# Reordering the first batches of an attention and MLP kernel: an earlier load of v, two attention outputs ahead of their scores, later loads gated on transposes

## The chip, the cores and the metric

The kernel runs on one core of a Trainium2 chip. The metric is device time in microseconds (us), as the median of several executions. Five engines work side by side, each through its own queue in program order: PE (matrix products), ACT (activation functions and copies), DVE (elementwise work and reductions), POOL (elementwise work, and the queue from which the loads are issued) and SP (a queue that only issues transfers). An engine whose next instruction waits does nothing else in the meantime.

## The reference, cut to what matters

Eight batches of eight heads go through a causal attention with a decay, and the result through an MLP with an exact GELU. S is 576, the head size 64, the model width 512, the hidden width 2048.

```python
scores = scale * np.matmul(q, k.transpose(0, 1, 3, 2))
cum = np.cumsum(np.maximum(s, 0.0), axis=-1)
bias = -(cum[:, :, :, None] - cum[:, :, None, :])
scores = np.where(causal, -1e9, scores + np.minimum(bias, 0.0))
attn = np.exp(scores - np.max(scores, axis=-1, keepdims=True))
attn = attn / (np.sum(attn, axis=-1, keepdims=True) + 1e-09)
x = np.matmul(attn, v)            # then [B, S, H * D]
...
h = x @ w_in
out = (0.5 * h * (1.0 + erf(h / np.sqrt(2.0)))) @ w_out
```

## The kernel before, in words

**What is computed where.** Heads go in pairs p = 0 to 3. Scores are made transposed, with exp of them in a tile P (two halves, "unit" 0 and 1), and the factor exp(cum) of the decay is put into v and into the weights of the row sum: `wb` holds exp(cum), `vv` holds v times `wb`. So an output is a numerator (vv times P) over a denominator (wb times P). The kernel works in bf16 and ends with a branch into a general version that this input does not take.

**Blocks.** After an opening (lines 583 to 645) that makes batch 0's attention, the loop over c (line 647) has nine blocks of 512 tokens. A block runs the first MLP product (`l1_item`, L519, eight pairs of hidden tiles) and then the second one (`l2_item`, L541, four groups "sub" of 128 tokens) cut into pieces, between which the attention of batch nb = c + 1 is put. The order on every engine is the order of the program text (`manual_schedule`, L86), so a line's place in the text is its place in each queue.

**The pieces of attention.**
- `tr_items` (L355) transposes q and k of a pair on PE (L366) into PSUM and copies them to `qkT` (L372), by ACT or DVE. It serves batches 0 and 1. From batch 2 on, `interleave` (L176) rearranges the loaded rows by four POOL copies (L180), `write_rows` (L187) writes them to DRAM from the SP queue, and `transpose_rows` (L194) brings them back transposed, eight transfers a batch, from the same queue.
- `sc_item` (L379) makes a pair's scores on PE, one unit at a time in one of two PSUM slots with the tag "sc", takes exp on ACT (L403), and zeroes the diagonal blocks on DVE (`mask_item`, L412 and L417). In the opening some items add a large negative number on PE instead (`neg=True`, L395).
- `av_item` (L479) makes a pair's denominator and numerator (L425), ln and exp of the denominator on ACT (`norm_act`, L441 and L442), and the product on DVE (`norm_dve`, L461) into xT, which `l1_item` of the next block reads. With `wide=True` the two lie in one "sc" slot, else in two slots with the tag "av".
- `scale_pair` (L580) makes `vv` of one pair on DVE (L232). `weights_dve` and `weights_pe` (L259 to L270) make cum and `wb`: one DVE operation, five transposes on PE, two exp on ACT.
- `keep_busy(n)` (L589) issues n products on zeros that nothing reads.

**Loads.** All loads of q, k, v and the weights are issued from POOL. `load_early(b, n, p)` loads half of q or k of a batch, `load_v` a batch's v in five slices, `load_w` a quarter of a weight. `pace` (L578) is a one-element POOL copy: what it reads must be there before POOL goes on to the loads behind it. Before the change it reads gT of the block from block 2 on (L665), which is written once the block's first GELU is done; at L717 and L746 it reads the last transposed k of a batch.

Of the kernel before, what the change touches and what calls it, by code (L numbers as in the profile page):

```python
# [19 lines left out]
def kernel(  # L20
# [10 lines left out]
    nc = tc.nc  # L31
# [12 lines left out]
    NP = H // 2  # L44
# [25 lines left out]
    MAIN = [(jt, i0, min(i0 + n, CUT) - i0, off) for jt, i0, n, u, off in SEGS if i0 < CUT]  # L70
# [86 lines left out]
    qkT = [const.tile([128, 2, NP, 640], bf16, name=f"qkT{i}") for i in range(2)]  # L157
# [101 lines left out]
    def weights_dve():  # L259
        nc.vector.tensor_scalar(cum, s_pos, s_pos[:, 287:288], None, op0=ALU.subtract)  # L260
# [160 lines left out]
    def av_mm(b, p, out, parts, den):  # L421
        for n_part, (jt, lo, n, off) in enumerate(parts):
            for e in range(2):
                h = 2 * p + e
                nc.tensor.matmul(  # L425
                    out[e * 64 : e * 64 + 64, lo : lo + n],
                    lhsT=(
                        wb[:, jt, b * H + h : b * H + h + 1].to_broadcast([128, 64])
                        if den else vv[b % 2][:, jt, h, :]
                    ),  # L430
                    rhs=P_of[b, p][:, e, off : off + n],
                    start=(n_part == 0), stop=n_part == len(parts) - 1,
                    skip_group_check=True,
                )
# [31 lines left out]
    def av_banks(wide=False, last=False):  # L466
        if wide:
            t = ps.tile([128, 2, 512], fp32, tag="sc", bufs=2, name="avw")
            return t[:, 0], t[:, 1]
        if last:  # L470
            num = ps.tile([128, 512], fp32, tag="mlp", bufs=1, name="avn")
            den = ps.tile([128, 512], fp32, tag="av", bufs=3, name="avd")
            return num, den
        den, num = [ps.tile([128, 512], fp32, tag="av", bufs=3, name=n) for n in ("avd", "avn")]
        return num, den
# [2 lines left out]

    def av_item(b, p, wide=False, rest=True):  # L479
        num, den = av_banks(wide)  # L480
        av_mm(b, p, den, MAIN, True)
        ln = norm_act(den, CUT, CHUNKS)
        av_mm(b, p, num, MAIN, False)
        if rest:
            av_rest(b, p)
        norm_dve(b, p, p + 1, num, ln, 0, CUT, CHUNKS)
# [14 lines left out]
    gT_of = {}  # L501
# [76 lines left out]
    pace = const.tile([128, 1], fp32, name="pace")  # L578

    def scale_pair(b, p):  # L580
        scale_v(b, ((0, ST - 1), (ST - 1, ST)), nc.vector, 2 * p, 2 * p + 2)
# [7 lines left out]
    def keep_busy(n):  # L589
        for _ in range(n):  # L590
            nc.tensor.matmul(warm, lhsT=busy[:, :128], rhs=busy, start=True, stop=True)  # L591
# [4 lines left out]
    keep_busy(3)  # L596
    sc_item(0, 0, masks=False)
    nc.vector.tensor_scalar(neg_bf, tri_bf, 2048.0, -2048.0, op0=MULT, op1=ALU.add)
    keep_busy(1)
    tr_items(0, 1, (0,))  # L600
    keep_busy(2)
    tr_items(0, 1, (1,))
    keep_busy(3)
    sc_item(0, 1, neg=True, units=(0,))
    tr_items(0, 2, (0,))
    keep_busy(1)
    tr_items(0, 2, (1,))
    weights_dve()
    sc_item(0, 1, neg=True, units=(1,))
    tr_items(0, 3, (0,))  # L610
    sc_item(0, 2, neg=True, units=(0,))
    weights_pe()
    tr_items(0, 3, (1,))
    sc_item(0, 2, neg=True, units=(1,))
    mask_item(0, 0, 0, nc.vector)
# [13 lines left out]
        load_early(1, n, 0)  # L629
    for i in range(4):  # L630
        load_w(1, i)
    for n in "qk":
        load_early(1, n, 2)
    load_v(1)
    load_qk(2)
    avs = {p: av_banks(p < 2, p == 3) for p in (2, 0, 1, 3)}
    for p in (2, 0, 1, 3):
# [9 lines left out]
    for c in range(NCH):  # L647
        nb = c + 1
        for k0, k1 in ((0, 2), (2, 3)) if c == 0 else ((0, 3),):
            l1_item(c, 0, k0, k1)  # L650
            l1_item(c, 1, k0, k1)
        l1_item(c, 0, KO - 1)
        l1_item(c, 1, KO - 1)
        l1_item(c, 2, av=True)
        if 0 < c and nb < B:
            scale_v(nb, STS, nc.vector)
            absmax_v(nb)
        if c == 0:
            absmax_v(0)
            scale_v(0, STS[ST - 1 :], nc.vector)  # L660
        if c < B:
            for p in range(NP):
                absmax(c, p)
        if 1 < c and nb + 1 < B:
            nc.gpsimd.tensor_copy(pace, gT_of[c][:, 0, 0:1])  # L665
            load_v(nb + 1)
            if nb + 2 < B:
                load_qk(nb + 2)
        for f2 in range(3, FT // 2):
            l1_item(c, f2)  # L670
        if c == 0:
            load_v(2)
            interleave(2, "q")
            interleave(2, "k")
            for p in range(NP):
                av_rest(0, p)
            tr_items(1, 0, (0, 1), wide=True)
            tr_items(1, 1, (0, 1), (nc.scalar.copy, nc.vector.tensor_copy), wide=True)
            exp_set()
            l2_item(c, 0, 0, 4)  # L680
            l2_item(c, 1, 0, 4, av=True)
            norm_rest(0)
            l2_item(c, 0, 4, 8)
            sc_item(1, 0)
            l2_item(c, 1, 4, 8, av=True)
            l2_item(c, 0, 8, 12)
            sc_item(1, 1)
            l2_item(c, 1, 8, 12, av=True)
            l2_item(c, 2, 0, 8, av=True)
            l2_item(c, 0, 12, copy=nc.scalar.copy)  # L690
            l2_item(c, 1, 12, av=True)
            tr_items(1, 2, (0, 1), (nc.scalar.copy, nc.vector.tensor_copy), wide=True)
            l2_item(c, 2, 8, 12, av=True)
            tr_items(1, 3, (0, 1), (nc.scalar.copy, nc.scalar.copy), wide=True)
            scale_pair(1, 0)
            l2_item(c, 2, 12, av=True)
            scale_pair(1, 1)
            l2_item(c, 3, 0, 4)
            sc_item(1, 2)
            av_item(1, 0, rest=False)  # L700
            scale_pair(1, 2)
            l2_item(c, 3, 4, 8)
            sc_item(1, 3)
            av_item(1, 1, rest=False)
            scale_pair(1, 3)
            write_rows(2, 0, nc.sync)
            l2_item(c, 3, 8, 12)
            av_item(1, 2, wide=True, rest=False)
            write_rows(2, 1, nc.sync)
            l2_item(c, 3, 12)  # L710
            av_item(1, 3, rest=False)
            for p in (0, 1):
                transpose_rows(2, p)
            gelu_set()
            for p in (2, 3):
                transpose_rows(2, p)
            nc.gpsimd.tensor_copy(pace, qkT[0][:, 1, 3, 0:1])  # L717
            load_qk(3)
            load_v(3)
            absmax_v(1)  # L720
        elif nb < B:
            exp_set()
            l2_item(c, 0, 0, 4)
            if c == 1:
                for p in range(NP):
                    av_rest(1, p)
            sc_item(nb, 0)
            if c == 1:
                norm_rest(1)
            l2_item(c, 0, 4)  # L730
            late = int(c == 1)
            for p in range(1, NP):
                if nb + 1 < B and p == 1 + late:
                    interleave(nb + 1, "q")
                    write_rows(nb + 1, 0, nc.sync)
                if nb + 1 < B and p > 1 and not late:
                    transpose_rows(nb + 1, p - 2)
                sc_item(nb, p)
                av_item(nb, p - 1)
                l2_item(c, p, 0, 12)  # L740
                if p == NP - 1:
                    if nb + 1 < B:
                        for pt in range(0 if late else p - 1, NP):
                            transpose_rows(nb + 1, pt)
                    if c == 1:
                        nc.gpsimd.tensor_copy(pace, qkT[(nb + 1) % 2][:, 1, p, 0:1])  # L746
                        load_qk(nb + 2)
                    av_item(nb, p)
                    norm_rest(nb)
                    gelu_set()  # L750
                l2_item(c, p, 12)
                if nb == B - 1 and p == 1:
                    cert_decay()
                if nb + 1 < B and p == 1 + late:
                    interleave(nb + 1, "k")
                    write_rows(nb + 1, 1, nc.sync)
        else:
            if c == B - 1:
                cert_1()
            for sub in range(4):  # L760
                if c == NCH - 1 and sub == 3:
                    l2_last(c, sub)
                    break
                l2_item(c, sub, av=sub % 2 == 0)
                if c == B - 1 and sub < 3:
                    (cert_2, cert_3, cert_4)[sub]()
# [151 lines left out]
```

## Time and profile before

| what | us |
|---|---|
| median of five runs (lowest to highest) | 331.78 (330.45 to 332.49) |
| the profiled execution, its time | 329.58 |
| its span, first to last instruction | 327.8 |
| opening, until the first product of block 0 starts | 0 to 21.06 |
| block 0, until block 1 goes on for good | 21.06 to 61.02 |
| block 1 | 61.02 to 95.28 |
| blocks 2 to 6 | 34.05 to 34.10 each |
| block 7, block 8 | 28.50, 33.70 |

The span is 1.78 us shorter than the time of its own execution, and that execution is 2.20 us below the median of the five. Times within the profile are us from the start of the span. A row of a timeline gives the start, the length, the engine, the line, what is written from what, and how many instructions were merged; in brackets stands how long the engine had been idle, and who ended that.

### The profile page before, as it was taken

To read this page: it belongs to the slowest core of one execution; us is meant where nothing else is said; L and a number is where in the kernel's file an instruction comes from. 1 tells how busy PE (TensorE), PEld (TensorE's weight loads), DVE (VectorE), ACT (ScalarE), POOL (GpSimd) and SP (SyncE) were. 2 spreads that over 40 slices of the span, in tenths; PEclk is the share of its full clock that TensorE was granted. 3 is DMA by queue.
4 is the path that set the end of the run, shared out by engine and by line. 5 is a ranking of instruction groups with operands and counts; after the bars stand their busy time and mean duration, and the time that the engine had idled before them with its cause. 6 is when DMAs were issued, how large, how long until landed. Compare 5 with 4: busy or idle time off the path is not lost.

```text
span 327.8 us, 8739 instructions
## 1 busy us (share of the span) xinstructions
PE 316.6 (97%) x3760; PEld 183.6 (56%) x3760; DVE 187.9 (57%) x356; ACT 204.9 (63%) x292; POOL 93.2 (28%) x124
## 2 busy tenths in 40 slices
PE   8999997899999999999999999999999999999992
PEld 3576655666665556546655665556555655455552
DVE  5777547995659366935494548644883672150021
ACT  4697758669576767677667767677759676105400
POOL 8744354407700970670058003700000000000000
PEclk9999999999999999999999999999999999999999
DMA  7999999967975899899689795627600100010012
GB/s 116 220 209 210 210 212 281 238 110 103 253 232 118 152 236 284 160 151 252 197 142 230 191 178 103 169 95 199 126 2 34 65 34 2 34 66 34 1 66 72
DMA packets 53838, 47.45 MB, mean 145 GB/s; under 512 B 31328, under 2 KB 43872, under 8 KB 53792
## 3 DMA queue, kind: packets, MB, share of 16 engines
q0 software_dynamic: 15936, 23.07, 38.0%
q1 hardware_dynamic: 37856, 23.75, 29.3%
q8 instruction: 31, 0.51, 0.7%
q14 instruction: 15, 0.12, 0.1%
HBM read 36.85 MB, written 16.52 MB: 163 GB/s over the span
## 4 chain that ended last, share of the span: by engine, by line
PE 94%; ACT 3%; DVE 1%; issue 0%
PE h_ps L519 38%; PE o_ps L541 37%; PE sc_ps L387 6%; PE avd L425 4%; PE avn L425 3%; PE warm L591 2%; ACT P L403 1%; PE tr_ps L366 1%; PE o_ps L562 1%; PE avr L425 1%; ACT ln L441 1%; DVE qkT L372 0%; PE sc_ps L395 0%; PE avw L425 0%; ACT gT L529 0%
## 5 line engine op out<-in xcount | busy, mean ns | idle before, releaser
L541 PE MATMUL o_ps<-w_out_r,gT 128*64 128x512 bf16 x1120 | 129.5, 380 | 0.0
L519 PE MATMUL h_ps<-xT,w_in_r 128*64 128x512 bf16 x1152 | 126.2, 379 | 0.7 <-DVE xT L461 0.7
L519 PEld LDWEIGHTS <-w_in_r 128*64 128x64 bf16 x1152 | 68.5, 110 | 56.4 <-issue 1.2
L541 PEld LDWEIGHTS <-gT 128*64 128x64 bf16 x1120 | 61.0, 110 | 49.6
L526 ACT ACTIVATE gT<-h_ps 128x1024 bf16<-128x1024 f32 x54 | 54.3, 1023 | 52.7 <-PE h_ps L519 52.7
L403 ACT ACTIVATE P<-sc_ps 128x1024 bf16<-128x1024 f32 x64 | 62.2, 1020 | 28.2 <-PE sc_ps L387 25.6
L412 DVE TENSOR_TENSOR P<-P,tri_bf 128x512 bf16<-128x512 bf16 x58 | 27.3, 477 | 47.4 <-ACT P L403 46.7
L548 DVE COPY o_sb<-o_ps 128x512 f32<-128x512 f32 x34 | 23.3, 686 | 47.6 <-PE o_ps L541 47.6
L215 DVE TENSOR_REDUCE amx<-qkT 128x2 f32<-128x1152 bf16 x32 | 40.9, 1335 | 0.0
L204 POOL DMA_DIRECT2D raw_v<-in_v_dram x40 | 34.2, 880 | 9.1 <-DMA w_out_r<-in_moe_w_out_dram 4.3
L461 DVE SCALAR_TENSOR_TENSOR xT<-avn,ln 128x256 bf16<-128x256 f32 (+3 forms) x66 | 22.4, 385 | 21.7 <-ACT ln L442 15.1
L232 DVE TENSOR_TENSOR vv<-raw_v,wb 128x512 bf16<-128x512 f32 (+3 forms) x44 | 26.8, 667 | 1.5 <-DMA raw_v<-in_v_dram 1.5
L442 ACT ACTIVATE ln<-ln 128x512 f32<-128x512 f32 (+1 forms) x40 | 23.5, 587 | 1.3
L222 DVE TENSOR_REDUCE amv<-raw_v 128x1 f32<-128x2048 f32 (+1 forms) x16 | 23.0, 1469 | 2.2 <-DMA raw_v<-in_v_dram 2.2
L441 ACT ACTIVATE ln<-avd 128x256 f32<-128x256 f32 x58 | 19.2, 391 | 7.6 <-PE avd L425 7.6
L529 ACT ACTIVATE gT<-h_ps 128x512 bf16<-128x512 f32 x36 | 19.6, 602 | 6.3 <-PE h_ps L519 6.3
L387 PE MATMUL sc_ps<-qkT 64*128 64x256 bf16 (+2 forms) x320 | 21.0, 250 | 0.5 <-ACT P L403 0.2
L387 PEld LDWEIGHTS <-qkT 64*128 64x128 bf16 x320 | 13.0, 94 | 14.9 <-issue 12.4
L425 PEld LDWEIGHTS <-vv 128*64 128x64 bf16 x384 | 17.7, 110 | 3.5 <-issue 2.6
L425 PEld LDWEIGHTS <-wb 128*64 128x64 bf16 x384 | 17.1, 110 | 4.1 <-issue 0.3
L665 POOL CAST pace<-gT 128x1 f32<-128x1 bf16 x4 | 1.9, 483 | 56.0 <-ACT gT L526 56.0
L425 PE MATMUL avd<-P,wb 128*64 128x256 bf16 x232 | 16.5, 263 | 0.0
(99 smaller groups left out, 188.2 us busy)
## 6 DMA issues: line engine op xcount, KB each, us to landing
out_dram<-o_sb SPq DMA_DIRECT2D x35, 256.0 KB, 3.5
raw_v<-in_v_dram POOLq DMA_DIRECT2D x32, 256.0 KB, 7.6
rows<-qk_bf SPq DMA_DIRECT2D x12, 576.0 KB, 5.1
early_q<-in_q_dram POOLq DMA_DIRECT2D x13, 288.0 KB, 10.2
early_k<-in_k_dram POOLq DMA_DIRECT2D x13, 288.0 KB, 10.8
w_in_r<-in_moe_w_in_dram POOLq DMA_DIRECT2D x4, 512.0 KB, 11.9
w_out_r<-in_moe_w_out_dram POOLq DMA_DIRECT2D x4, 512.0 KB, 15.1
raw_v<-in_v_dram POOLq DMA_DIRECT2D x8, 128.0 KB, 9.2
```

What stands on the lines that cost most here:

```text
L204: nc.gpsimd.dma_start(out=t[:n_st, st, :, :], in_=bass.AP(tensor=v.tensor, offset=v.offset + b * H * S * D + st * 128 * D, ap=[[D, n_st], ...
L215: nc.vector.tensor_reduce(amx[:, b * NP + p], qkT[b % 2][:, :, p, :S], axis=AX, op=ALU.max, apply_absolute_value=True)
L232: eng.tensor_tensor(vb[:n_st, st0:st1, h0:h1, :], t[:n_st, st0:st1, h0:h1, :], wb[:n_st, st0:st1, b * H + h0 : b * H + h1] .unsqueeze(3).t ...
L387: nc.tensor.matmul(s_ps[:, e, off : off + n], lhsT=qkT[b % 2][e * 64 : e * 64 + 64, 1, p, jt * 128 : jt * 128 + 128], rhs=qkT[b % 2][e * 6 ...
L403: nc.scalar.activation(P[:, :, UO[u] : UO[u] + UW[u]], s_ps[:, :, : UW[u]], func=AF.Exp, scale=scale)
L412: eng.tensor_tensor(d, d, tri_bf.unsqueeze(1).unsqueeze(1).to_broadcast([128, 2, 2, 128]), op=MULT)
L425: nc.tensor.matmul(out[e * 64 : e * 64 + 64, lo : lo + n], lhsT=(wb[:, jt, b * H + h : b * H + h + 1].to_broadcast([128, 64]) if den else ...
L442: nc.scalar.activation(ln[:, :w], ln[:, :w], func=AF.Exp, scale=-1.0)
L519: nc.tensor.matmul(h_of[c, f2][i][e * 64 : e * 64 + 64], lhsT=w_in_r[:, ko, ft * 128 + e * 64 : ft * 128 + e * 64 + 64], rhs=xT[:, ko, c * ...
L526: nc.scalar.activation(gT_of[c][:, f2 * 2 : f2 * 2 + 2, :], hh_of[c, f2], func=AF.Gelu)
L541: nc.tensor.matmul(o_ps[e * 64 : e * 64 + 64], lhsT=gT[:, ft, t0 : t0 + 64], rhs=w_out_r[:, ft, :], start=(ft == 0), stop=(ft == FT - 1), ...
L548: (copy or nc.vector.tensor_copy)(o_sb, o_ps)
```

## The change

Three places. In the opening, `weights_dve` and `weights_pe` come before the transposes of the second half of pair 1, the first half of pair 2 is transposed before pair 1's scores, and 15 fillers are left of 20. In the loads, v of batch 1 is issued ahead of the second q and k half of batch 1, and the one-element copy at L665 reads the last transposed k of batch nb in place of gT. In block 0, outputs (1, 0) and (1, 1) are made before the scores of pairs 2 and 3, with their `scale_pair` ahead of them; the transposes of pairs 2 and 3 come later; sub 2 of the second product runs through in one piece and is copied out by ACT; the k half of pair 3 is copied by DVE. `av_item` with `wide=True` makes the numerator before the denominator.

```diff
--- before.py
+++ after.py
@@ -478,9 +478,12 @@
 
     def av_item(b, p, wide=False, rest=True):
         num, den = av_banks(wide)
+        if wide:
+            av_mm(b, p, num, MAIN, False)
         av_mm(b, p, den, MAIN, True)
         ln = norm_act(den, CUT, CHUNKS)
-        av_mm(b, p, num, MAIN, False)
+        if not wide:
+            av_mm(b, p, num, MAIN, False)
         if rest:
             av_rest(b, p)
         norm_dve(b, p, p + 1, num, ln, 0, CUT, CHUNKS)
@@ -596,20 +599,18 @@
     keep_busy(3)
     sc_item(0, 0, masks=False)
     nc.vector.tensor_scalar(neg_bf, tri_bf, 2048.0, -2048.0, op0=MULT, op1=ALU.add)
+    weights_dve()
     keep_busy(1)
     tr_items(0, 1, (0,))
-    keep_busy(2)
+    weights_pe()
     tr_items(0, 1, (1,))
-    keep_busy(3)
+    keep_busy(1)
+    tr_items(0, 2, (0,))
     sc_item(0, 1, neg=True, units=(0,))
-    tr_items(0, 2, (0,))
-    keep_busy(1)
     tr_items(0, 2, (1,))
-    weights_dve()
     sc_item(0, 1, neg=True, units=(1,))
+    sc_item(0, 2, neg=True, units=(0,))
     tr_items(0, 3, (0,))
-    sc_item(0, 2, neg=True, units=(0,))
-    weights_pe()
     tr_items(0, 3, (1,))
     sc_item(0, 2, neg=True, units=(1,))
     mask_item(0, 0, 0, nc.vector)
@@ -629,9 +630,9 @@
         load_early(1, n, 0)
     for i in range(4):
         load_w(1, i)
+    load_v(1)
     for n in "qk":
         load_early(1, n, 2)
-    load_v(1)
     load_qk(2)
     avs = {p: av_banks(p < 2, p == 3) for p in (2, 0, 1, 3)}
     for p in (2, 0, 1, 3):
@@ -662,7 +663,7 @@
             for p in range(NP):
                 absmax(c, p)
         if 1 < c and nb + 1 < B:
-            nc.gpsimd.tensor_copy(pace, gT_of[c][:, 0, 0:1])
+            nc.gpsimd.tensor_copy(pace, qkT[nb % 2][:, 1, NP - 1, 0:1])
             load_v(nb + 1)
             if nb + 2 < B:
                 load_qk(nb + 2)
@@ -689,22 +690,21 @@
             l2_item(c, 2, 0, 8, av=True)
             l2_item(c, 0, 12, copy=nc.scalar.copy)
             l2_item(c, 1, 12, av=True)
+            scale_pair(1, 0)
+            scale_pair(1, 1)
+            l2_item(c, 2, 8, av=True, copy=nc.scalar.copy)
+            av_item(1, 0, rest=False)
+            l2_item(c, 3, 0, 4)
             tr_items(1, 2, (0, 1), (nc.scalar.copy, nc.vector.tensor_copy), wide=True)
-            l2_item(c, 2, 8, 12, av=True)
-            tr_items(1, 3, (0, 1), (nc.scalar.copy, nc.scalar.copy), wide=True)
-            scale_pair(1, 0)
-            l2_item(c, 2, 12, av=True)
-            scale_pair(1, 1)
-            l2_item(c, 3, 0, 4)
+            scale_pair(1, 2)
+            av_item(1, 1, rest=False)
+            tr_items(1, 3, (0, 1), (nc.scalar.copy, nc.vector.tensor_copy), wide=True)
+            scale_pair(1, 3)
+            l2_item(c, 3, 4, 8)
             sc_item(1, 2)
-            av_item(1, 0, rest=False)
-            scale_pair(1, 2)
-            l2_item(c, 3, 4, 8)
+            l2_item(c, 3, 8, 12)
             sc_item(1, 3)
-            av_item(1, 1, rest=False)
-            scale_pair(1, 3)
             write_rows(2, 0, nc.sync)
-            l2_item(c, 3, 8, 12)
             av_item(1, 2, wide=True, rest=False)
             write_rows(2, 1, nc.sync)
             l2_item(c, 3, 12)
```

## Prediction

> **What bounds the kernel now.** I read the page first, then the busy time by stretches, PE's waits, and the timeline of the stretch that stands out.
>
> ```profile
> PE 316.6 (97%) x3760; PEld 183.6 (56%) x3760; DVE 187.9 (57%) x356; ACT 204.9 (63%) x292; POOL 93.2 (28%) x124
> ```
>
> PE sets the end, so only time in which PE stands still can be won. By stretches (length, then PE's busy time first):
>
> ```profile
> 0.00:21.06 21.06, 18.73 (x292) 11.03 (x293) 13.69 (x32) 13.80 (x21) 15.29 (x30) 1.00 0.99 177
> 21.06:61.02 39.96, 36.94 (x545) 22.89 (x541) 25.75 (x46) 28.89 (x45) 19.49 (x24) 1.00 1.13 227
> 61.02:95.28 34.26, 34.23 (x420) 22.10 (x421) 25.02 (x41) 23.67 (x35) 12.02 (x15) 1.00 0.87 194
> 95.28:129.33 34.05, 34.05 (x395) 19.37 (x392) 22.91 (x37) 23.88 (x35) 13.95 (x19) 1.00 0.87 180
> ```
>
> Opening and block 0 hold 2.3 and 3.0 us of idle PE, the later blocks none: there the change can only lose. PE's waits name the places:
>
> ```profile
> PE avw L425 <- ACT ln L441: 2.5, 2, 2.1
> PE h_ps L519 <- DVE xT L461: 0.7, 1, 0.7
> ```
>
> and the timeline around the longest, PE, DVE and POOL:
>
> ```profile
> 57.72 0.57 PE L425 MATMUL avw<-P,vv 128*64 128x256 bf16 x8 [2.10 <-ACT ln L441]
> ...
> 61.02 0.41 PE L519 MATMUL h_ps<-xT,w_in_r 128*64 128x512 bf16 x2 [0.66 <-DVE xT L461]
> ```
> ```profile
> 57.83 2.47 DVE L232 TENSOR_TENSOR vv<-raw_v,wb 128x512 bf16<-128x512 f32 x2
> 60.23 0.74 DVE L461 SCALAR_TENSOR_TENSOR xT<-avw,ln 128x256 bf16<-128x256 f32 x2
> ```
> ```profile
> 56.38 2.24 POOL L180 COPY qk_bf<-early_q 128x1152 bf16<-128x1152 bf16 x2 [3.14 <-DMA early_q<-in_q_dram]
> 58.55 2.76 POOL L180 COPY qk_bf<-early_k 128x1152 bf16<-128x1152 bf16 x2
> ```
>
> The numerator of output 2 waits for the ln of its own denominator, because both lie in one PSUM tile. Then block 1 waits for xT, which stood on DVE behind a scale_pair of 2.47 us; earlier ones took 0.88. It ran under POOL's interleave copies (about 1.12 each). Block 1 did four products (0.43) before its stop, so it starts in effect at 61.02 - 0.43 = 60.59. That is the number to beat.
>
> **What the Trainium skill says.** "SBUF — State Buffer", section "SBUF: two separate sides": VectorE and GpSimd share a port pair under an exclusive lock; a VectorE operation with two SBUF inputs and a GpSimd operation that reads SBUF shut each other out for whole instructions. The trace agrees: the masks (L412, two SBUF inputs, 0.42 alone) took up to 2.84 under interleave copies (119.98), PSUM reads did not slow (an output copy at 84.48 took 0.69). "DMA: Bandwidth & Descriptors", section "Issuing engines are not separate DMA queues": writes from SP share the engines with POOL's loads. Agrees: v's slices landed 1.0 to 1.2 us apart, 1.8 and 2.2 once output writes had begun at 46.72. "TensorE: Matmul & The Clock Gate", section "Why this matters for your kernels": the clock falls after PE gaps beyond some 3 us. No gap here is that long; the granted clock is 1.00 in every stretch above.
>
> **Part 1, the opening.** Five fillers go (about 0.22 each, 1.1 in all), but they lie in gaps in which PE waits for exps; they are worth nothing. The end is set by ACT: eight exps of P at 1.02, with the two exps of wb (0.38 + 0.21) between the fifth and the sixth, and idle times of 1.51, 0.81 and 0.16. The wb exps move to 9.25, into the idle 1.51: that takes 0.5 off the chain. Pair 2's first transposes move ahead of pair 1's scores; their rows land at 4.07 + 5.0 = 9.07 and 4.65 + 5.2 = 9.85, before their new places (9.4, 10.7), and the 0.81 before pair 1's second exp mostly closes. New small waits (0.1, 0.35 and 0.15 before later exps) take some back. Stepping the queues with these lengths, the last exp ends at 17.3 in place of 18.1, and block 0 starts at 20.3: **gain 0.75**. The moved DVE operation (0.50) fits in DVE's idle 1.21 before 8.24; without that cover pair 1's first copy is 0.3 later.
>
> **Part 2, the order of the loads.** From issue plus time to landing, before: last w_out 41.2; q, k half 42.3 and 44.0; v slices 44.9, 46.1, 47.9, 50.1, 50.9. DVE waited for the fourth until 50.29. After: v follows w_out at some 1.07 a slice (0.55 for the short one), landing at 46.1, mostly before the first output write. The half then competes with output writes; batch 2's halves under such writes landed 1.4 and 1.6 apart, so it lands at 49.2. If no work is saved by the new order it is 50.9, and 51.8 with sub 2's write now ahead of it. I take at most 49.5. POOL issues the same number; the others keep their places.
>
> **Part 3, block 0's tail.** With the 0.75, sub 1 ends at 46.1, sub 2's eight remaining tiles at 47.85, output 0 (0.8; its vv is done at 47.6 on DVE behind sub 1's copy) at 48.65, four tiles of sub 3 at 49.5. There the transposes of pair 2 need the half, so X = 49.5. Then by queue: DVE does copy, scale_pair 2, product of output 1, and only then pair 3's k copy, until X + 4.2. That copy frees the slot for unit 1 of pair 2's scores: PE stands still 1.5 (a **new wait** on the engine that got the copy from ACT). Exps of pair 2 and 3 follow to X + 7.7; output 2 waits 0.8 for a slot; the masks of pair 3 end at X + 8.4 = 57.9, output 3 is made, and block 1 starts at 58.85. The wide swap removes the 2.10 wait, at no cost; what is late next is the masks. ACT's load is the same but for sub 2's copy (0.59), taken while it idles.
>
> That is 1.74 better than 60.59, if the masks run alone. They don't: the interleave copies begin when batch 2's q has landed (56.38 before; 54 to 56.5 after), four of 1.12 in a row. In the trace each DVE operation with two SBUF inputs that met them waited for at least one: the three masks at 85.87 to 88.8 lost 1.6 in all, those at 119.98 lost 2.4. Before, scale_pair paid; now pair 3's three masks do, with output 2's product behind them on DVE. Delay d: 1.5 gives 60.0, 2.4 gives 61.0, one whole copy for each mask (3.2) gives 61.8. I take d = 2.2, block 1 at **60.8, a loss of 0.2**. So the 0.75 and the 2.10 are both spent on one collision.
>
> **Part 4, the held loads.** From block 3 on, v and q, k loads wait for the transposes: x6 of them took 13.20 at 134.52 beside loads, 7.71 at 163.14 without. So they end at 142.8, land 1.85 later, loads are issued for 6.9 and the interleave starts at 151.6 in place of 140.9; in block 4 at 182.5 in place of 174.95. Behind POOL's wait stand loads needed a block later (v at 165, needed landed; it lands near 157) and the interleave, whose rows reach SP's queue by 156.7 in place of 154.2; pair 0 of batch 5 is needed at 178.2 and is there by 167. All hidden. But the interleave leaves the MLP stretch, where it met only absmax (one SBUF input), and comes under the masks. I price that at 0.2 in block 4 (free slot for the next output late behind DVE), bounds 0 and 1.6; a gain is excluded, since PE has no idle there.
>
> **Sum.** 0.2 + 0.2 = +0.4 on 329.58 for the profiled execution, 330.0; the median of the five lies 2.2 higher, so 331.78 + 0.4 = **332.2**. About 0.3% (1.0 us) is what a measurement of this kernel can tell from no change, so I forecast no change.
>
> **The rivals.**
> - A, the forecast: d from 1.5 to 3.2, so -0.6 to +1.4. For it: every overlap in the trace cost a copy per operation. 331.2 to 333.2; chance 0.45.
> - B, faster: the masks get through, because the interleave starts after 57.3 or VectorE wins the lock. Against: loads of before put it at 56.38. Block 1 at 58.9 to 59.2, -1.4 to -1.7: **330.2**; chance 0.28.
> - C, slower: the held loads bring block 4's interleave onto the masks of pair 0. There the denominator starts at 182.12 and the last mask ends at 182.33: no slack. It decides once the copies start before 181.8; I put them at 182.5. Price 1.6, as at 85.87, on top of A: **333.8**; chance 0.17.
> - D, the q, k half lands at 51.8, so the moved transposes stop PE for 2.3 and part 3 slides: block 1 at 61.9, 1.3 late, **333.1**; chance 0.10.
>
> **How the numbers follow.** Faster by over 0.3%: B, 0.28. Slower: C, most of D, and the end of A with d near 3 (0.10): 0.35. The rest is 0.37. The range runs from below B's middle to just below C, 330.0 to 333.6; C's chance and a little of B and D are left out. A's own range is 331.2 to 333.2.
>
> **What would show it.** Right: the last exp of the opening near 17.3; no avw wait on ln; DVE's wait for v gone; a PE wait on qkT before pair 2's second unit of scores; pair 3's masks lengthened under L180; x6 transposes in block 3 near 8 us. Wrong: masks at 0.42 with POOL copying, or block 1 before 60, or PE waits in blocks 3 to 5.

## The result and the profile after

The changed kernel takes **334.6 us** (median of 42 runs, 331.77 to 340.42), the kernel before 331.47 (79 runs beside it, 329.66 to 342.69). The ratio is **1.0076, 95% interval 1.0060 to 1.0092**: slower by 0.8%, about 2.5 us. The ratio compares the runs of each kernel that lie within 1.5% of its fastest; medians and ranges are of all runs. The forecast was 332.2, "no change", with 330.0 to 333.6 as its range.

The profiled execution of after took 335.23 us (span 333.4), 0.6 above its median; that of before lies 1.9 below its own. So the two traces stand 5.65 us apart and the medians 3.1: a part of what the traces show is not in every run. Still, even the shortest of the 42 lies above the median of before. Where a comparison below rests on the time, the medians and ratios are used, and the traces say only where it went.

The page's line of engines, as the first thing: PE's busy time has hardly grown (316.6 before), its share has fallen from 97 to 95%. So PE stands still more.

```profile
PE 317.5 (95%) x3755; PEld 186.6 (56%) x3755; DVE 201.2 (60%) x356; ACT 205.2 (62%) x292; POOL 92.8 (28%) x124
```

Next the busy time by stretches, cut at the first product of each block of after (length, then busy time and instruction count of PE, PEld, DVE, ACT, POOL, then the share of its full clock that PE was granted, DMA share, GB/s):

```profile
0.00:20.10 20.10, 17.18 (x287) 10.29 (x288) 14.14 (x32) 13.73 (x21) 14.91 (x30) 1.00 1.01 179
...
94.92:129.92 35.00, 34.37 (x395) 19.88 (x392) 24.05 (x37) 23.83 (x35) 13.94 (x19) 1.00 0.91 178
129.92:163.99 34.07, 34.07 (x394) 21.16 (x392) 23.75 (x36) 23.99 (x35) 11.71 (x14) 1.00 0.88 182
163.99:198.11 34.12, 34.12 (x395) 19.40 (x393) 23.77 (x39) 24.01 (x36) 11.54 (x14) 1.00 0.86 175
198.11:237.10 38.99, 35.84 (x395) 20.69 (x392) 24.79 (x37) 23.98 (x35) 9.04 (x10) 0.96 0.66 141
```

A block of the steady part takes 34.05. **Block 5 takes 38.99**: PE is idle in 3.15 of it, and its clock is 0.96 on the mean. Block 2 takes 0.95 longer than that. The other blocks are as before. Summed from the block starts: the opening gives 0.96 (block 0 starts at 20.10, not 21.06); of that 0.36 is left when block 1 goes on for good (60.66 - 0.43 = 60.23 against 60.59); block 2 loses 0.95, block 5 loses 4.94, the rest 0.03. That makes 5.56 of the 5.65.

PE's waits name who is late (total, times, longest):

```profile
PE avd L425 <- DVE P L412: 3.5, 3, 3.0
PE sc_ps L387 <- DVE qkT L372: 1.5, 2, 1.1
PE avw L425 <- ACT P L403: 1.2, 2, 0.9
```

The 2.1 on the ln is gone, as forecast. In its place stands a wait of 3.0 on one mask (L412), and the group of that line has gone from 477 to 661 ns on the mean:

```profile
L412 DVE TENSOR_TENSOR P<-P,tri_bf 128x512 bf16<-128x512 bf16 x58 | 37.7, 661 | 44.9 <-ACT P L403 44.3
```

One mask makes 2.96 of the 3.5. The timeline of block 5, POOL first, then DVE, then PE (start, length):

```profile
211.77 0.19 POOL L666 CAST pace<-qkT 128x1 f32<-128x1 bf16 x1 [20.82 <-DMA qkT<-rows]
212.31 4.26 POOL L204 DMA_DIRECT2D raw_v<-in_v_dram  x5 [0.35 <-issue]
216.53 2.26 POOL L180 COPY qk_bf<-early_q 128x1152 bf16<-128x1152 bf16 x2
218.70 2.46 POOL L180 COPY qk_bf<-early_k 128x1152 bf16<-128x1152 bf16 x2
```
```profile
216.50 3.67 DVE L412 TENSOR_TENSOR P<-P,tri_bf 128x512 bf16<-128x512 bf16 x1 [0.38 <-ACT P L403]
220.09 1.16 DVE L417 TENSOR_TENSOR P<-P,tri_bf 128x128 bf16<-128x128 bf16 x1
```
```profile
220.22 0.53 PE L425 MATMUL avd<-P,wb 128*64 128x256 bf16 x4 [2.96 <-DVE P L412]
```

To be read from top to bottom: the pace copy now waits for the last transpose (`<-DMA qkT<-rows`, 20.82 of idle); v's loads take POOL for 4.26 more; then the four interleave copies start at 216.53, within 0.03 of a mask of batch 6's pair 0. That mask, 0.42 when alone, takes 3.67: three copies start ahead of it (216.53, 217.62, 218.70), and it ends at 220.17, when the fourth has just begun (219.79). The next mask waits for that one (1.16). The denominator's product on PE waits 2.96 for the first. In the kernel before, the same copies ran from 206.61 to 211.02, done 4 us before the first mask of pair 0 (214.97):

```profile
206.61 2.24 POOL L180 COPY qk_bf<-early_q 128x1152 bf16<-128x1152 bf16 x2
208.78 2.24 POOL L180 COPY qk_bf<-early_k 128x1152 bf16<-128x1152 bf16 x2
```

How regular this is shows in a count over the masks of all twelve traces of this case (before, after and the ten experiments). The 650 that meet no work of POOL take 0.42 (128x512) or 0.22 (128x128) to within 0.01. Of the 100 that meet copies alone, 87 take over 0.2 longer. Of the 112 that meet only the issue of q, k loads, 9 do, by up to 0.98: so the copies are the rule, but not the only work of POOL that can hold up a mask.

What follows on PE is as dear as half the wait itself. Stretches of 3 us around it:

```profile
217.00:220.00 3.00, 0.26 (x4) 0.09 (x1) 3.00 (x1) 1.68 (x2) 3.00 (x4) 1.00 0.80 165
220.00:223.00 3.00, 2.59 (x26) 1.99 (x27) 3.00 (x8) 1.29 (x3) 1.16 (x1) 0.52 0.10 35
223.00:226.00 3.00, 3.00 (x28) 1.72 (x24) 0.31 (x1) 0.00 (x0) 0.00 (x0) 0.91 0.68 249
```

After the stop the granted clock is 0.52, then 0.91: 3 x 0.48 + 3 x 0.09 = 1.7 us lost. With the wait of 2.96 and one of 0.19 for a free output slot that is 4.9, so all but 0.1 of block 5's 4.94.

### The profile page after: what moved, and what is told of

The parts are those of the page before. It is cut to its first block, busy times and chain, and to the rows that moved or that the text cites. A ratio compares the mean times of both kernels' runs of the same rounds, so it can differ in the third digit from the quotient of the medians.

```text
span 333.4 us, 8728 instructions
## 1 busy us (share of the span) xinstructions
PE 317.5 (95%) x3755; PEld 186.6 (56%) x3755; DVE 201.2 (60%) x356; ACT 205.2 (62%) x292; POOL 92.8 (28%) x124
## 4 chain that ended last, share of the span: by engine, by line
PE 76%; DMA 11%; POOL 3%; DVE 3%; issue 3%; ACT 2%; POOLq 0%; DVEq 0%
PE h_ps L522 33%; PE o_ps L544 31%; DMA w_out_r<-in_moe_w_out_dram 5%; PE sc_ps L387 4%; DMA early_k<-in_k_dram 4%; PE avd L425 3%; PE avn L425 3%; DMA w_in_r<-in_moe_w_in_dram 2%; ACT P L403 1%; DVE P L412 1%; PE o_ps L565 1%; POOL raw_v L204 1%; PE avr L425 1%; POOL early_q L117 1%; POOL early_k L117 1%
## 5 line engine op out<-in xcount | busy, mean ns | idle before, releaser
L522 PEld LDWEIGHTS <-w_in_r 128*64 128x64 bf16 x1152 | 70.2, 110 | 54.6 <-issue 1.1
L544 PEld LDWEIGHTS <-gT 128*64 128x64 bf16 x1120 | 62.3, 111 | 50.0 <-issue 1.1
L412 DVE TENSOR_TENSOR P<-P,tri_bf 128x512 bf16<-128x512 bf16 x58 | 37.7, 661 | 44.9 <-ACT P L403 44.3
L551 DVE COPY o_sb<-o_ps 128x512 f32<-128x512 f32 x33 | 22.6, 685 | 48.0 <-PE o_ps L544 47.9
L232 DVE TENSOR_TENSOR vv<-raw_v,wb 128x512 bf16<-128x512 f32 (+3 forms) x44 | 25.2, 631 | 0.1
L425 PE MATMUL avd<-P,wb 128*64 128x256 bf16 x232 | 17.1, 265 | 3.5 <-DVE P L412 3.5
L666 POOL CAST pace<-qkT 128x1 f32<-128x1 bf16 x4 | 0.8, 195 | 64.3 <-DMA qkT<-rows 64.3
```

Source lines behind the costliest of these rows:

```text
L232: eng.tensor_tensor(vb[:n_st, st0:st1, h0:h1, :], t[:n_st, st0:st1, h0:h1, :], wb[:n_st, st0:st1, b * H + h0 : b * H + h1] .unsqueeze(3).t ...
L412: eng.tensor_tensor(d, d, tri_bf.unsqueeze(1).unsqueeze(1).to_broadcast([128, 2, 2, 128]), op=MULT)
L425: nc.tensor.matmul(out[e * 64 : e * 64 + 64, lo : lo + n], lhsT=(wb[:, jt, b * H + h : b * H + h + 1].to_broadcast([128, 64]) if den else ...
L522: nc.tensor.matmul(h_of[c, f2][i][e * 64 : e * 64 + 64], lhsT=w_in_r[:, ko, ft * 128 + e * 64 : ft * 128 + e * 64 + 64], rhs=xT[:, ko, c * ...
L544: nc.tensor.matmul(o_ps[e * 64 : e * 64 + 64], lhsT=gT[:, ft, t0 : t0 + 64], rhs=w_out_r[:, ft, :], start=(ft == 0), stop=(ft == FT - 1), ...
```

## The experiments

All were timed in five rounds beside the kernel before on the same chip. A ratio is against that kernel.

### The hold undone, and the hold alone

My theory after the first look was that the held loads (part 4) cost it all, and that parts 1 to 3 come out even. Two kernels cross the parts. The first is after with the old pace:

```diff
-            nc.gpsimd.tensor_copy(pace, qkT[nb % 2][:, 1, NP - 1, 0:1])
+            nc.gpsimd.tensor_copy(pace, gT_of[c][:, 0, 0:1])
```

> The changed kernel with one line undone: the one-element copy ahead of the later loads reads gT of the block again, in place of the last transposed k. Theory (gate): holding the loads brings the interleave copies of block 5 onto the masks of batch 6's pair 0, PE stops for 3 us there and its clock is low for some 4 us afterwards. Then this kernel keeps the opening's and block 0's 0.4 us and loses at most block 2's 0.9: between 0.5 us faster and 0.6 us slower than before, no PE wait over 1 us behind block 0. Rival (block 2 and the clock state come from the earlier start of block 1 alone, and block 5 too): as slow as the changed kernel, 2 to 5 us slower than before.

The second is before with the new pace and nothing else:

```diff
-            nc.gpsimd.tensor_copy(pace, gT_of[c][:, 0, 0:1])
+            nc.gpsimd.tensor_copy(pace, qkT[nb % 2][:, 1, NP - 1, 0:1])
```

> The kernel before with only the gate: the copy ahead of the later loads reads the last transposed k. Gate theory: 1.5 to 5 us slower than before, with a PE wait on a mask in block 4 or 5. Rival: no change, within 0.5 us of before, since opening, loads and block 0 are those of before.

Measured:

| | old opening and block 0 | new opening and block 0 |
|---|---|---|
| old pace | 331.2 (before) | 330.85, ratio 0.9992 (0.9969 to 1.0015) |
| new pace | 335.56, ratio 1.0100 (1.0037 to 1.0164) | 334.6, ratio 1.0076 (1.0060 to 1.0092) |

The hold costs 0.8 to 1.0% with either opening. The rest of the change can't be told from nothing. The hold alone rests on six runs, so its interval is wide. In its trace it isn't block 5 that is hit but blocks 3 and 4. PE's waits and, in block 3, DVE's mask:

```profile
PE avn L425 <- DVE xT L461: 2.1, 1, 2.1
PE avd L425 <- DVE P L412: 2.1, 1, 2.1
```
```profile
151.34 4.40 DVE L417 TENSOR_TENSOR P<-P,tri_bf 128x128 bf16<-128x128 bf16 x1
```

A mask of 128x128, 0.22 when alone, took 4.40: it began at 151.34, while POOL still issued q, k loads (until 152.34), and ended at 155.74, three copies later (the third ends at 155.65). So the hold brings the copies within reach of the masks in blocks 3, 4 and 5. Which of them is hit in an execution seems to hang on some hundred nanoseconds; that fits the spread of the runs, but no run shows two executions of one kernel hit in different blocks.

The kernel with the old pace shows what the hold does good. With the loads beside them the six transposes on SP's queue take 14.15 (8.47 in after), and in block 3 PE waits for their rows:

```profile
PE sc_ps L387 <- DMA qkT<-rows: 1.9, 1, 1.9
```

With the clock that followed, that block took 37.67, so the expected "no PE wait over 1 us behind block 0" was missed. This execution (333.77) is the second longest of the kernel's 22; its median was as expected.

### The hold undone in block 5 alone

```diff
-            nc.gpsimd.tensor_copy(pace, qkT[nb % 2][:, 1, NP - 1, 0:1])
+            nc.gpsimd.tensor_copy(pace, gT_of[c][:, 0, 0:1] if c == 5 else qkT[nb % 2][:, 1, NP - 1, 0:1])
```

> The held loads are released early again in block 5 alone; blocks 2 to 4 keep the new hold. My theory (in block 5 the hold brings POOL's interleave copies onto the masks of batch 6's pair 0, and PE stands still 3 us and then runs at half its clock): block 5 falls from 38.99 to 34.05, the interleave starts near 206, the time is 4.9 below after's 334.6, 329.7. Rival (the loss in block 5 comes from the work of block 5 being late through the earlier holds, whatever POOL does in it): a PE wait of over 1 us in block 5 stays and the time stays above 332.5.

Measured: 331.47 (329.34 to 336.92, 22 runs), ratio 1.0004 (0.9981 to 1.0028). Block 5 by stretches and POOL in it:

```profile
197.12:231.17 34.05, 34.05 (x395) 19.36 (x393) 20.77 (x37) 23.87 (x35) 9.17 (x10) 1.00 0.81 158
```
```profile
206.26 2.27 POOL L180 COPY qk_bf<-early_q 128x1152 bf16<-128x1152 bf16 x2
208.43 2.26 POOL L180 COPY qk_bf<-early_k 128x1152 bf16<-128x1152 bf16 x2
```

With the copies back at 206 PE has no idle in block 5; the rival, that block 5 is late whatever POOL does there, falls. The profiled execution took 329.34, the shortest of its 22. The ratio fell from 1.0076 to 1.0004, which is 2.4 us and not 4.9: the theory's place is right and its size holds for the profiled executions only. The longer runs of this kernel were not profiled; the copies are still held in blocks 3 and 4 (151.25 and 184.55 in its trace), so a hit there is the likely reason, not a shown one.

### Shorter copies: how long is a mask shut out?

The forecast took one copy for each mask as the dearest case. In the 3.67 a single mask lost three. Either VectorE (DVE) lost three times in a row by chance, or it stays shut out while GpSimd (POOL) has more to run. In block 5 each copy is cut in three:

```diff
+        step = 3 if b == 7 else G
         for j in range(2):
-            nc.gpsimd.tensor_copy(
-                t[:, j].rearrange("g r e d -> g e r d"),
-                early[b, n][:, j].rearrange("g e (r d) -> g e r d", r=G),
-            )
+            for r in range(0, G, step):
+                nc.gpsimd.tensor_copy(
+                    t[:, j].rearrange("g r e d -> g e r d")[:, :, r : r + step],
+                    early[b, n][:, j].rearrange("g e (r d) -> g e r d", r=G)[:, :, r : r + step],
+                )
```

> The last interleave, in block 5, is cut from four copies of 128x1152 into twelve of 128x384; the hold stays. Theory 1 (VectorE, once it has lost the shared port to GpSimd, stays shut out until GpSimd's run of copies ends): the mask still takes over 3 us, PE still waits about 3, time 334.6 as after. Theory 2 (a waiting VectorE operation loses one GpSimd instruction, whatever its length, and the 3.67 was chance): the mask takes 0.42 plus one short copy of about 0.4, so below 1.2; PE waits below 0.7; block 5 near 34.6 and the time near 330.2.

Measured: 332.78 (329.45 to 337.52, 12 runs), ratio 1.0048 (1.0019 to 1.0078); the profile is of an execution of 336.01, the third longest of the twelve, so it shows what can happen and not what is usual. POOL, DVE and PE in block 5:

```profile
216.19 2.74 POOL L182 COPY qk_bf<-early_q 128x384 bf16<-128x384 bf16 x6
218.86 2.94 POOL L182 COPY qk_bf<-early_k 128x384 bf16<-128x384 bf16 x6
```
```profile
216.14 4.21 DVE L419 TENSOR_TENSOR P<-P,tri_bf 128x128 bf16<-128x128 bf16 x1
```
```profile
220.40 0.27 PE L427 MATMUL avr<-P,vv 128*64 128x64 bf16 x2 [3.30 <-DVE P L419]
```

A 128x128 mask took 4.21 us under copies of about 0.52 each, started 0.45 apart: nine of them passed ahead of it (the ninth ends at 220.27, the mask at 220.35). Block 5 took 40.56. So what decides isn't the length of one copy, and cutting the copies doesn't let the mask in. In this trace the second theory falls. The first holds in its number, but not to the letter: like the mask in after, this one got in before the run's end (221.80), after some 4 us. What ends a shut-out is open. The time lies between the two forecasts (334.6 and 330.2), which fits a stop that not every execution has in full; how often it comes the runs don't say.

### The copies moved off the masks

The hold is kept. In the first kernel the interleave stands ahead of the pace copy on POOL from block 3 on; in the second also block 2's goes ahead of its q, k loads, and block 5's waits for that block's first gT. The calls further down, in the loop over the pairs, fall away for these blocks.

```diff
         if 1 < c and nb + 1 < B:
+            if 2 < c:
+                interleave(nb + 1, "q")
+                interleave(nb + 1, "k")
             nc.gpsimd.tensor_copy(pace, qkT[nb % 2][:, 1, NP - 1, 0:1])
...
```

> The changed kernel, gate kept, but from block 3 on the interleave copies stand in POOL's queue ahead of the gate and its loads, so that they run in the MLP stretch at the start of a block. If it is the meeting of copies and masks that costs, blocks 3 to 6 last 34.05 again, no mask is longer than 0.5 us there, and the kernel is 0.4 us faster than before to 0.6 us slower (block 2 is left as it is). If holding the loads costs by itself (late v or late transposes), it stays 2 us slower or more.

```diff
         if 1 < c and nb + 1 < B:
+            if c == 5:
+                nc.gpsimd.tensor_copy(pace, gT_of[c][:, 0, 0:1])
             if 2 < c:
                 interleave(nb + 1, "q")
                 interleave(nb + 1, "k")
             nc.gpsimd.tensor_copy(pace, qkT[nb % 2][:, 1, NP - 1, 0:1])
             load_v(nb + 1)
+            if c == 2:
+                interleave(nb + 1, "q")
+                interleave(nb + 1, "k")
             if nb + 2 < B:
                 load_qk(nb + 2)
...
```

> All that the change does is kept, the hold too, but in block 2 the interleave goes ahead of the q, k loads, in blocks 3 and 4 ahead of the hold, and in block 5 to that block's start. Theory (the copies on the masks are the whole loss of blocks 2 to 5): every block from 2 to 6 takes 34.05 to 34.3; against the kernel with the interleave ahead from block 3 on (330.88) 0.6 less in block 2 and 0.8 less in block 4, so 329.5. Rival (the holds cost something of their own, late transposes or rows written later): a PE wait on a DMA or on qkT in blocks 2 to 5, and no less than 330.9.

Measured: 330.88 (22 runs), ratio 0.9995 (0.9972 to 1.0018), and 330.39 (14 runs), ratio 0.9991 (0.9974 to 1.0008). The first has its time as expected, but not every block: block 4 took 34.90, where copies from 194.10 on still met two masks (1.00 and 1.16). In the second, blocks 2 to 5 take 34.06, 34.63, 34.12 and 34.05; 34.63 lies outside the forecast. Its stop of 0.41 on PE stands behind two masks (159.84 and 160.57) under copies that began at 159.23. All 14 runs lie between 329.40 and 331.41, where those of after spread over 8.6 us; only 7 of the 49 runs of before beside it were above 334, so that none of 14 was may be chance. So the hold itself costs nothing that these runs can tell once POOL's copies keep off most masks, and the rival of late rows falls: no PE wait on a DMA or on qkT in these blocks. The hoped-for 329.5 was not reached: against the first kernel the ratio moved by 0.0004, less than its interval, in place of 1.4 us.

### What the opening and block 0 are worth

The opening alone, put into the kernel before (the second hunk of the change's diff, whole; here its core):

```diff
+    weights_dve()
     keep_busy(1)
     tr_items(0, 1, (0,))
-    keep_busy(2)
+    weights_pe()
     tr_items(0, 1, (1,))
-    keep_busy(3)
+    keep_busy(1)
+    tr_items(0, 2, (0,))
     sc_item(0, 1, neg=True, units=(0,))
...
```

> The kernel before with the change's opening alone: decay exponentials first, pair 2's first transposes ahead. Theory (the opening's gain carries through only as far as a later stage isn't set by something else): block 0 starts 0.96 earlier, at 20.1; the loads of the middle stay where they were, so DVE's wait for v and the collision at the end of block 0 hold part of it back, and block 1 starts between 59.2 and 59.7 (59.73 before): 0 to 0.5 gained, 330.7 to 331.2. Rival (nothing in block 0 is tied to the loads): block 1 at 58.8 and 0.9 gained, 330.3.

Measured: 330.87 (14 runs), ratio 0.9998 (0.9972 to 1.0025). Block 0 starts at 20.25, 0.81 earlier, and block 1 at 60.29 (60.59 in effect before). PE there, and the stretches of 3 us after it:

```profile
56.92 0.57 PE L425 MATMUL avw<-P,vv 128*64 128x256 bf16 x8 [2.09 <-ACT ln L441]
```
```profile
57.00:60.00 3.00, 3.00 (x29) 2.36 (x30) 3.00 (x6) 0.68 (x2) 3.00 (x3) 0.58 0.87 261
60.00:63.00 3.00, 3.00 (x30) 2.06 (x27) 2.41 (x5) 2.42 (x4) 0.36 (x1) 0.85 0.80 307
```

In this execution the old wait on the ln cost not only its 2.09 but the clock after it, so that 0.3 was left; block 2 then lost 0.8 (34.86) with copies at 119.35, and block 2 ended later than before. In time nothing was gained that can be told from zero, within the theory's 0 to 0.5. Its start of block 1 was missed: the first product came at 60.29, where 59.2 to 59.7 was forecast (59.73 before). The rival's 58.8 is further off still.

Block 2's 0.95 in after is the same kind of meeting. One mask near 119.6 waits there behind batch 4's copies. In after and in before:

```profile
119.10 2.24 POOL L180 COPY qk_bf<-early_q 128x1152 bf16<-128x1152 bf16 x2
119.62 4.17 DVE L412 TENSOR_TENSOR P<-P,tri_bf 128x512 bf16<-128x512 bf16 x1 [0.69 <-ACT P L403]
```
```profile
118.14 2.24 POOL L180 COPY qk_bf<-early_q 128x1152 bf16<-128x1152 bf16 x2
119.98 2.84 DVE L412 TENSOR_TENSOR P<-P,tri_bf 128x512 bf16<-128x512 bf16 x1 [0.69 <-ACT P L403]
```

In eight traces this mask meets these copies, and in each the block loses what the mask takes beyond 3.22: 0.96 of 4.18 (old pace), 0.95 of 4.17 (after), 0.81 of 4.03 (opening alone), 0.63 of 3.85 (interleave ahead from block 3 on), 0.18 of 3.40 (hold undone in block 5), nothing of 2.99 (short copies), 2.84 (before) and 2.50 (hold alone). So the loss doesn't need the hold. It comes with parts 1 to 3 and with the opening alone (in after this mask starts 0.4 earlier and the copies 1.0 later, 119.10 for 118.14), but not in every execution: four of the eight (after, interleave ahead, hold undone in block 5, short copies) have one and the same order up to block 2 and lose 0.95, 0.63, 0.18 and 0.

The other way about, batch 2's interleave in block 0 is put behind the last mask of batch 1:

```diff
             load_v(2)
-            interleave(2, "q")
-            interleave(2, "k")
...
             sc_item(1, 3)
+            nc.gpsimd.tensor_copy(pace, P_of[1, 3][:, 1, PW - 1 : PW])
+            interleave(2, "q")
+            interleave(2, "k")
             write_rows(2, 0, nc.sync)
```

> The changed kernel, with batch 2's interleave copies in block 0 put behind a one-element POOL copy that reads the end of pair 3's masked P of batch 1, so that these masks run before the copies. Theory of block 0: the three masks end 2 us earlier, and block 1 starts in effect at 58.3 to 58.8 in place of 60.23, a gain of 1.5 to 2 us up to there; the transposes of batch 2 come 2 us later, with slack. Rival (something else is late next, such as ln and exp on ACT): block 1 starts less than 0.7 earlier. The end depends on where block 5's copies then fall: 1 to 5 us slower than before, or faster if they miss the masks.

Measured: 340.85 (6 runs), ratio 1.0246 (1.0188 to 1.0305); the profiled execution is the longest of the six (342.17). Pair 3's masks at the end of block 0, and PE's waits:

```profile
56.21 0.42 DVE L412 TENSOR_TENSOR P<-P,tri_bf 128x512 bf16<-128x512 bf16 x1 [0.75 <-ACT P L403]
57.12 0.42 DVE L412 TENSOR_TENSOR P<-P,tri_bf 128x512 bf16<-128x512 bf16 x1 [0.49 <-ACT P L403]
57.46 0.22 DVE L417 TENSOR_TENSOR P<-P,tri_bf 128x128 bf16<-128x128 bf16 x1
```
```profile
PE avd L425 <- DVE P L412: 6.0, 5, 2.3
```

With the masks alone block 1 starts at 58.62 and has no stop: this is the 58.85 of the prediction's part 3. So the opening and block 0 do hold 1.6 us (60.23 - 58.62) that the collision there takes. But then blocks 2 to 5 take 37.15, 37.82, 36.55 and 38.67, in all 14 us above 34.05 each, with a mask of 3.3 to 4.9 in each of the four. Block 2 starts 1.0 earlier than in after (93.90 for 94.92), batch 4's copies come later (123.78 for 119.10), and so they meet the masks of the next pair. The gain of 1.6 is lost several times over.

### Two tries at a faster kernel

The late copies of batch 2 and the off-mask version together, with block 2's copies gated between the masks of two pairs, each in its old place in the loop over the pairs:

```diff
+                    if c == 2:
+                        nc.gpsimd.tensor_copy(pace, P_of[nb, 0][:, 1, PW - 1 : PW])
                     interleave(nb + 1, "q")
...
+                    if c == 2:
+                        nc.gpsimd.tensor_copy(pace, P_of[nb, 1][:, 1, PW - 1 : PW])
                     interleave(nb + 1, "k")
```

> The kernel with the interleaves of blocks 3 to 5 moved off the masks, and the last two that still met them moved too: batch 2's waits in block 0 until the last mask of batch 1 is made, and in block 2 each of batch 4's two halves waits until the masks of a pair are made, so that it runs in the 3.5 us before the next pair's. Theory (nothing but copies on masks takes back what the opening and the order of the loads give): block 1 starts at 58.6 without a stop, in place of 60.47 in effect; block 1 takes 35.3, blocks 2 to 6 34.05 to 34.6; 1.2 less than the 330.39 of before's off-mask version, 329.2, and 0.5% below the kernel before. Rival (the later rows and transposes of batches 2 and 4 become a wait, as every placement so far has moved the stop on): a PE wait on qkT or on a DMA in blocks 2 or 3 of over 0.5, and 330.4 or more.

Measured: 333.24 (22 runs), ratio 1.0041 (1.0016 to 1.0065). Block 1 starts at 58.86 as the theory has it, but block 2 takes 36.61. POOL had stood in the q, k loads until 123.8, so both gates were long open, and the copies met pair 3's masks after all:

```profile
124.41 4.64 DVE L412 TENSOR_TENSOR P<-P,tri_bf 128x512 bf16<-128x512 bf16 x2 [0.69 <-ACT P L403]
```

The rival, a wait of over 0.5 on qkT or a DMA in blocks 2 or 3, doesn't appear; copies on a mask are again what costs.

In the second the gates come one pair later and read `P_of[nb, 1]` and `P_of[nb, 2]`, and block 2's loads stand behind the copies:

```diff
-        if 1 < c and nb + 1 < B:
+        if 2 < c and nb + 1 < B:
...
-            late = int(c == 1)
+            late = int(c in (1, 2))
...
                     write_rows(nb + 1, 1, nc.sync)
+                    if c == 2:
+                        load_v(nb + 1)
+                        load_qk(nb + 2)
```

> As the kernel with the interleaves between the masks, but in block 2 batch 4's q copies wait for the masks of pair 1 and its k copies for those of pair 2, and the loads of v (batch 4) and q, k (batch 5) go behind them on POOL, where before POOL stood in the load instructions until 123.7 and the gates were long open. Theory: block 2 takes 34.05 to 34.3 in place of 36.61, with no wait on a mask there, and the profiled time is 2.3 to 2.5 below 331.8, near 329.4. Rival: the loads behind the copies land too late, and block 3 shows a wait on v, qkT or rows; 331 or more.

Measured: 331.4 (328.58 to 335.72, 22 runs), ratio 0.9977 (0.9948 to 1.0005). Block 2 takes 34.04, as the theory says; block 3 takes 39.36, as the rival says, in a profiled execution of 334.46, the second longest of the 22:

```profile
PE sc_ps L387 <- DMA qkT<-rows: 2.6, 1, 2.6
```

The loads, issued from 124.91 on, now lie beside block 3's transposes (from 128.68 on), which is what the hold was there to avoid. Its shortest run, 328.58, is the shortest of all, but its interval includes 1; a version that is reliably faster was not found.

## Why the prediction was wrong

- **Part 1, right.** The gain was 0.96 for 0.75; the opening's last exp of P ends at 17.1, forecast 17.3.
- **Part 2, right where it was needed.** The q, k half landed at 49.48 ("at most 49.5"), and DVE no longer waits for v. The last slice of v came at 47.23, not 46.1, and nothing waited for it.
- **Part 3, right in mechanism.** The new wait before pair 2's second unit is 1.06 (forecast 1.5), output 2's wait 0.90 (0.8). Pair 3's masks end at 59.94; alone they would let block 1 start at 58.62 (58.85). The delay is 1.6 where d was 2.2, and block 1 starts in effect at 60.23, a gain of 0.36 in place of a loss of 0.2. (58.85 + 2.2 is 61.05; the 60.8 comes out only as 57.9 + 2.2 with some 0.7 of DVE work behind the masks, a term that isn't written down.) Not seen was that moving the masks against the copies by 1.4 could cost up to 0.95 in block 2. The kernel with the old pace (0.9992) bears out parts 1 to 3 as "no change", but that is luck in part: at block 1 they came out 0.56 better than forecast, and in block 2 up to 0.95 worse.
- **Part 4 failed**, at "I price that at 0.2 in block 4 ..., bounds 0 and 1.6". Its mechanism, the interleave leaving the stretch of the MLP and coming under the masks, is the cause. But the 0.2 was to be the whole loss of blocks 3 to 6, and the hold cost 0.8 to 1.0% (2.8 to 3.3 us) in the runs, 4.94 in block 5 of after's trace. Three things in the step were wrong.
  - *The place.* Block 5 was never stepped. It could have been: before, the copies of block 5 come 31.66 after those of block 4 (206.61 - 174.95), since no q, k loads are left to issue. From the prediction's own 182.5 that gives 214.2 to 218.7, and the masks of pair 0, one block of 34.05 after 182.12 to 182.33, stand at 216.2 to 216.4. So its own numbers put an overlap one block behind the near miss at which the step stopped. To the microsecond that would have been luck, since block 4's copies came at 186.26, 3.8 later than forecast. In after's trace the copies of blocks 3 (153.00) and 4 lengthened masks too, to 1.36 at most, which cost PE nothing; the hold alone shows PE stopped in both.
  - *The price of a hit.* 1.6 was read from three masks that lost it together, no one of them more than about a copy. One mask can lose three in a row: it took 3.67 in after, 4.40 and 4.21 elsewhere, and PE then waits 2 to 3.3. The trace of before had a warning. The prediction speaks of "those at 119.98", but it was one mask that lost 2.4 there (2.84 for 0.42), waiting behind the rest of one copy and two whole ones.
  - *The clock.* "No gap here is that long" was true of before only. A hit stopped PE for 2.96 in after, and the 1.7 of lost clock came on top; gaps of 1.89 to 2.11 were enough in other traces (below).
- **The rivals.** C, given 0.17, had the mechanism and the sign; its place (block 4) and its price were wrong, so that its 333.8 lies near 334.6 is luck. A (0.45) needed part 4 at 0.2. B and D did not happen.
- **The range** ended at 333.6, just below C with its 1.6, and so left out every dear hit. With one such mask in one of the three blocks, 3 of wait and 1.7 of clock on the forecast's 332.2, it would have reached 337 (an estimate from after's trace).

On the Trainium skill's "SBUF — State Buffer", section "SBUF: two separate sides": it says that the operation that starts first has the shared pair for its whole instruction. The traces agree on the lock and add what it doesn't say: with further copies queued on GpSimd, the loser is not always next in line (nine copies of 0.52 passed ahead of one mask).

## What to carry to other kernels

When a wait is added to a queue, step every block in which the moved work runs, the last ones too, where a missing load changes the phase; a near miss in one block is a hit in another. Price a collision for an exclusive resource, at its dearest, at nearly the whole run of the other engine's instructions, not at one of them, and add the clock that a stopped PE loses. Ask also how much slack the waiting work has: in block 2 masks of up to 3.22 cost nothing. Where two engines meet like that, move them apart in their queues: the version that did so in blocks 2 to 5 was not faster than before, but its 14 runs lay within 2 us, which may be chance. A gate that ties the copies to a mask helps only where they don't then run into the masks behind it, as the kernels with late copies and with copies between the masks show.

## What the runs showed of the hardware

- **A VectorE operation with two SBUF inputs can be starved by a run of GpSimd copies**: 0.42 became 3.67 under copies of 1.1 to 1.2, 0.22 became 4.40 under the end of a run of q, k load issues and three such copies, and 4.21 under short ones. At other times one copy was lost only (1.16 at 220.09). The issue of q, k loads alone can do it too: a mask at 150.88 in after took 1.16 for 0.22 with no copy running (the first came at 153.00).
- **A PE gap of 2 us can cost the clock, or not.** A granted clock of 0.50 followed gaps of 2.96 (after), 2.60 (the second of the two tries), 2.11 (hold alone, block 3), 2.09 (opening alone) and 1.89 (old pace); 1.00 stayed after 2.10 (before, and hold alone in block 4) and 2.27 (batch 2's copies late). The Trainium skill's "TensorE: Matmul & The Clock Gate", section "What's actually happening", says that activity is judged in free-running windows of about 3.4 us, so that the moment of a switch varies with the phase. The traces agree: each low stretch before a kernel's end lasts 3.41 or twice that, and where a trace has several they start a whole number of 3.41 apart. Counted off in such steps, the hold alone's 2.11 lies whole in one (154.29 to 157.70), and its 2.10 is split over two, 1.46 and 0.64. Over all traces, a step at full clock with at most 1.49 of idle PE was followed by full clock, one with 2.11 or more by 0.50, and from 1.69 to 1.94 both occur. So the idle share of a step says more than the length of the gap. That a step idle for some 2 of its 3.41 is enough is less than the page's one idle window, and there the measurement decides.
- **Transposes beside loads**: six on SP's queue took 14.15 (old pace), and 8.47 with the loads held (after).
